# A blank first round of TensorE's loop, split first loads and early branch hints in an attention kernel

## The chip, the cores and the metric

The kernel runs on one core of one Trainium2 chip. The metric is the time of an execution on the device in microseconds (us). Times quoted as a kernel's time are medians of several executions. The profile's span is some 1.5 to 2 us shorter than the same execution's time, because it leaves out what lies before the first and after the last recorded instruction.

## The reference

```python
B, H, Sq, Sk, D = 16, 32, 192, 1024, 128        # q, k, v are bf16

def reference(q, k, v):
    scale = q.shape[-1] ** -0.5
    scores = jnp.einsum("bhqd,bhkd->bhqk", q, k) * scale
    p = _softmax(scores, axis=-1)
    return jnp.einsum("bhqk,bhkd->bhqd", p, v)
```

512 heads, each with 192 queries against 1024 keys. The kernel takes four heads at a time (a group x, 128 groups in all), cuts a group into three pieces, and calls a piece f (384 in all).

## The kernel before

SyncE loads K and V (1 MB each for a group) and Q. VectorE and GpSimd turn K into the layout that the matmul needs, TensorE computes scores (QK), ScalarE the exponentials (e1, e3), TensorE the product with V (PV) four pieces later, VectorE normalises, and the result is stored. The code that the change touches is this, with cuts marked.

```python
            def _(e):                                    # SyncE: the loads
                def load_k(x):
                    if x >= NKN:                         # NKN = 5 buffers
                        e.wait_ge(s_kx, 3 * (x - NKN) + 3)
                    e.dma_start(kn[:, x % NKN, :],
                        kf[4 * x:4 * x + 4].rearrange("a (j r) d -> (a j) (r d)", r=32).bitcast(U32),
                    ).then_inc(s_kn[x % NKN], 16)
                # ... load_q, load_v alike
                k0 = kf[0:4].rearrange("a (j s t) d -> (a j) s (t d)", s=4, t=8).bitcast(U32)
                # ...
                e.dma_start(kn0[:, :, 0:cut], k0[:, :, 0:cut]).then_inc(s_k0, 16)
                load_q(0)
                e.dma_start(kn0[:, :, cut:], k0[:, :, cut:]).then_inc(s_kn[0], 16)
                load_k(1)
                # ... the loads of the following groups, then all the rest, the last stores
                for so in range(NSO):
                    e.wait_ge(s_st[so], 16 * len(range(so, len(stores), NSO)))
```

TensorE's program is one loop of 64 rounds. Each round holds two groups (six pieces). The second half of one PV stands at the head of the next round, so that the jump back falls inside a PV:

```python
                with nc.Fori(0, NF // (3 * R), engines=[mybir.EngineType.PE],
                             head_slot={mybir.EngineType.PE: 100}):
                    pv(-1 - LAG, (1,))
                    for f in range(3 * R):
                        qk(f)
                        pv(f - LAG, (0,) if f == 3 * R - 1 else (0, 1))
```

At the end a flag says whether some row sum was out of range. Each engine loads the flag and branches over a general path that recomputes everything; the branch is taken here:

```python
            with eng.register() as r:
                eng.reg_load(r, redo[0:1, 0:1])
                with eng.If_ne(r, 0):
                    body(eng)
```

## Time and profile before

| kernel before | value |
|---|---|
| time, median of 3 runs | 828.15 us (826.99 to 828.18) |
| span of the profile | 826.16 us |
| first exponential of piece f9 starts at | 38.25 us |
| one round of TensorE's loop, median | 12.420 us |
| from the flag (VectorE's last conversion) to the end of the span | 6.71 us |

I use the start, the rounds and the tail as the ledger. The start of f9 says how well the start went: by then the instructions and the first groups are there, so what comes after is the steady loop. The round is read from the loop's counter instruction, which runs once a round. The tail is what comes after all the work is done. A group line of the profile gives busy time and the mean of one instruction in ns, and after the second bar the idle time just before such instructions with what ended most of it.

### The profile page before, as it was taken

The page shows a single profiled execution, that of the slowest core. Times are in us where ns is not written, and L with a number is a line of the kernel's source. Part 1 is how long each engine was busy: PE and PEld are TensorE (multiplying, and loading weights), DVE is VectorE, ACT ScalarE, POOL GpSimd, SP SyncE. Part 2 cuts the span into 40 slices and gives each one's busy share as a digit, 9 for nine tenths or more (in the row PEclk, how much of TensorE's full clock was granted, in tenths as well). Part 3 has the DMA queues.
Part 4 walks back from the last instruction along what each step waited for, and adds up shares of the span by engine and source line. Part 5 has one row for each costly group of instructions (what it writes and reads, how often), then busy time and mean ns, then how long its engine had stood idle before and what let it go on. Part 6 is the DMA issues. An engine that isn't in the chain of part 4 may idle for free. (4 is left out here: it accounts for less than half of the span.)

```text
span 826.2 us, 71554 instructions
## 1 busy us (share of the span) xinstructions
PE 807.5 (98%) x32926; PEld 717.1 (87%) x32926; DVE 599.8 (73%) x1288; ACT 748.5 (91%) x770; POOL 550.4 (67%) x646
## 2 busy tenths in 40 slices
PE   6899999999999999999999999999999999999995
PEld 4788888888888888888888888888888888888885
DVE  5477777777777777777777777777777777777773
ACT  5699999999999999999999999999999999999994
POOL 6566766766766666667667667666676676676671
PEclk9899999999999999999999999999999999999998
DMA  8999999999999999999999999999999999999951
GB/s 326 398 405 406 406 406 406 407 405 407 407 404 407 405 406 405 403 404 405 401 401 406 399 405 400 399 402 405 399 402 400 403 400 404 397 401 401 402 167 44
DMA packets 139214, 319.22 MB, mean 386 GB/s; under 512 B 7200, under 2 KB 57376, under 8 KB 122912
## 3 DMA queue, kind: packets, MB, share of 16 engines
q1 hardware_dynamic: 106432, 294.41, 91.0%
q10 hardware_dynamic: 32736, 24.38, 8.8%
q14 instruction: 40, 0.33, 0.1%
q8 instruction: 6, 0.10, 0.1%
HBM read 293.60 MB, written 25.17 MB: 386 GB/s over the span
## 5 line engine op out<-in xcount | busy, mean ns | idle before, releaser
L783 ACT ACTIVATE f_pt<-f_s 128x1536 bf16<-128x1536 f32 x384 | 554.6, 1444 | 3.3 <-PE f_o L636 3.3
L571 POOL COPY f_kt<-f_kx 128x768 uint32<-128x768 uint32 (+1 forms) x384 | 294.0, 785 | 255.6 <-DVE f_kx L699 137.3
L636 PE MATMUL f_o<-f_vp,f_pt 128*64 128x129 bf16 x12336 | 424.9, 222 | 3.4 <-issue 3.3
L614 PE MATMUL f_s<-f_qt,f_kt 32*128 32x192 bf16 (+2 forms) x20480 | 422.0, 226 | 5.6 <-PEq L597 3.4
L636 PEld LDWEIGHTS f_o<-f_vp,f_pt 128*64 128x64 bf16 x12336 | 365.3, 110 | 54.7 <-issue 25.5
L614 PEld LDWEIGHTS f_s<-f_qt,f_kt 32*128 32x128 bf16 x20480 | 347.5, 92 | 42.1 <-issue 6.5
L699 DVE STREAM_TRANSPOSE f_kx<-f_kn 128x768 uint32<-128x768 uint32 (+1 forms) x384 | 334.1, 871 | 10.1 <-DMA f_kn<-in_k_dram 10.1
L780 ACT ACTIVATE f_pt<-f_s 128x512 bf16<-128x512 f32 x384 | 229.3, 597 | 62.0 <-PE f_s L614 32.3
L580 POOL COPY f_vp<-f_vs 128x1024 uint32<-128x1024 uint32 x256 | 259.7, 1044 | 5.0 <-PE f_o L636 4.8
L720 DVE RECIPROCAL f_rinv<-f_o 128x2 f32<-128x2 f32 x381 | 65.1, 171 | 192.9 <-PE f_o L636 192.9
L724 DVE TENSOR_TENSOR f_ob<-f_o,f_rinv 128x256 bf16<-128x256 f32 x381 | 161.7, 424 | 13.3 <-DVE f_rinv L720 0.3
L708 DVE STREAM_TRANSPOSE f_qt<-f_qn 128x384 uint32<-128x384 uint32 x128 | 72.8, 569 | 0.0
L661 PE MATMUL f_o<-f_ones 128*128 128x512 bf16 x12 | 4.2, 528 | 1.1 <-POOL f_ones L562 1.1
L661 PEld LDWEIGHTS f_o<-f_ones 128*128 128x128 bf16 x12 | 1.5, 130 | 3.3 <-issue 1.9
L563 POOL MEMSET f_vp<- 128x4352 uint32 x1 | 3.7, 3729 | 0.0
L680 DVE MEMSET f_pt<- 128x3072 uint32 x1 | 2.6, 2618 | 1.5 <-PEq L811 1.5
L636 PE MATMUL f_s<-f_vp,f_pt 128*64 128x129 bf16 x96 | 3.1, 220 | 0.4 <-PEq L597 0.4
L636 PEld LDWEIGHTS f_s<-f_vp,f_pt 128*64 128x64 bf16 x96 | 2.8, 110 | 0.5 <-issue 0.5
L772 ACT ACTIVATE f_pt<-f_ones 128x3072 f32<-128x3072 bf16 x1 | 2.8, 2762 | 0.0
L772 ACT ACT_TABLE_LOAD x1 | 1.3, 1283 | 0.8 <-PEq L811 0.8
L720 DVE RECIPROCAL f_rinv<-f_s 128x2 f32<-128x2 f32 x3 | 0.5, 171 | 1.4 <-PE f_s L636 1.4
L674 PE MATMUL f_o<-f_bad,f_ones 128*1 128x1 bf16 x1 | 0.2, 164 | 1.3 <-DVEq L764 1.3
(13 smaller groups left out, 5.3 us busy)
## 6 DMA issues: line engine op xcount, KB each, us to landing
f_vs<-in_v_dram SPq DMA_DIRECT2D x128, 1024.0 KB, 10.9
f_kn<-in_k_dram SPq DMA_DIRECT2D x127, 1024.0 KB, 13.2
f_qn<-in_q_dram SPq DMA_DIRECT2D x128, 192.0 KB, 13.1
out_dram<-f_ob ACTq DMA_DIRECT2D x62, 384.0 KB, 9.5
f_kn<-in_k_dram SPq DMA_DIRECT2D x1, 640.0 KB, 7.0
f_kn<-in_k_dram SPq DMA_DIRECT2D x1, 384.0 KB, 3.9
out_dram<-f_ob SPq DMA_DIRECT2D x1, 384.0 KB, 3.3
out_dram<-f_ob SPq DMA_DIRECT2D x2, 192.0 KB, 2.1
```

The source lines that it names most:

```text
L571: gp.tensor_copy(kt[:, x % NKT].bitcast(U32).rearrange("p U (j s u) c -> p U j s (u c)", s=2, u=2)[:, lo:hi], kx[:, x % 2].rearrange("p (U ...
L580: gp.tensor_copy(vp[:, x % NVP, 2 * T * i: 2 * T * i + 2 * T, 0:D].bitcast(U32), vs[:, x % NVS, 2 * i: 2 * i + 2, :].rearrange("p a (t d) ...
L614: ins = pe.matmul(S[:, c0: c0 + n1 - n0], kt[r, x % NKT, 2 * t + h, :, c], qt[r, x % R, h, n0:n1, c], start=w == 0 and g == 0, stop=w == 3 ...
L636: return pe.matmul(O[m0: m0 + m, u, 0:129], pt[:, x % R, 2 * y + z, t * SQ + n0: t * SQ + n0 + m], vp[:, x % NVP, (2 * y + z) * T + t, 0:129],
L661: pe.matmul(o_ps[:].rearrange("p a b -> p (a b)"), ones[:], ones[:].unsqueeze(1).to_broadcast([128, 4, 128]), start=True, stop=True)
L699: dve.transpose(kx[:, x % 2].rearrange("p (U s j u) -> p s u U j", s=2, j=32, u=2)[:, :, :, lo:hi], kn[:, x % NKN].rearrange("p (s u U i) ...
L708: dve.transpose(qt[:, x % R].bitcast(U32).rearrange("p b (y j u) c -> p u y b (j c)", y=3, u=2), qn[:, x % NKN].rearrange("p (u y b i) -> ...
L720: dve.reciprocal(ri, O[:, :, 128]).then_inc(s_rc, 1)
L724: dve.tensor_tensor(ob[:, so, 6 * a + 2 * w: 6 * a + 2 * w + 2, :], O[:, :, 0:128], ri.unsqueeze(2).to_broadcast([128, 2, D]), ALU.mult,). ...
L772: act.activation(pt[:, 1].rearrange("p a c -> p (a c)").bitcast(F32), ones[:, 0:1].to_broadcast([128, 2 * T * SQ]), ACT_FN.Copy).then_inc( ...
L780: act.activation(pt[:, x % R, 0, c], s1_ps[:], ACT_FN.Exp, scale=scale).then_inc(s_e1, 1)
L783: act.activation(pt[:, x % R, 1:4, c], s3_ps[f % 2][:], ACT_FN.Exp, scale=scale).then_inc(s_e3, 1)
```

## The change

There are three intents. TensorE's loop gets one more round at first, which does no work: it jumps from the head to a label in the middle and from there to one at the end, in order to have the instruction blocks fetched before the DMA queues fill. The first loads are cut (K in halves, V in quarters), K of the first group becomes an ordinary load, and the first Q goes out on ScalarE's queue. At the end, each engine gets a branch hint well ahead of its branch, and SyncE waits for the last stores after its branch instead of before it. Two waits move along: TensorE's for Q to the loop's head, and the one for the tiles that are filled at the start from TensorE to VectorE. The diff, cut to its core:

```diff
-                with eng.If_ne(r, 0):
+                eng.br_ne(r, 0, on_true=name + "_do", on_false=name + "_end").branch_hint(hints[eng.engine])
 ...
+            sync_general(e)
+            stored(e)
 ...
+    SPLIT_K, SPLIT_V = 2, 4
 ...
+                    n = SPLIT_K if x < NKN else 1
+                    for i in range(n):
+                        e.dma_start(
+                            kn[128 // n * i: 128 // n * (i + 1), x % NKN, :],
+                            kf[4 * x + 4 // n * i: 4 * x + 4 // n * (i + 1)].rearrange(
+                                "a (j r) d -> (a j) (r d)", r=32).bitcast(U32),
+                        ).then_inc(s_kn[x % NKN], 16)
 ...
+                            vs[:, x % NVS, 4 // n * i: 4 // n * (i + 1), :],
 ...
+                load_k(0)
                 load_k(1)
 ...
+                pe.reg_mov(first, 1)
+                def skip(here, there):
+                    pe.br(here)
+                    nc.switch_bb(here, parent=top[0])
+                    pe.br_ne(first, 0, on_true=there, on_false=here + "_on")
+                    nc.switch_bb(here + "_on", parent=top[0])
 ...
-                with nc.Fori(0, NF // (3 * R), engines=[mybir.EngineType.PE],
+                with nc.Fori(0, NF // (3 * R) + 1, engines=[mybir.EngineType.PE],
                              head_slot={mybir.EngineType.PE: 100}):
+                    skip(tag + "_open", tag + "_mid")        # "_mid" lies inside the QK of f4
+                    take(s_qt, 1)
                     pv(-1 - LAG, (1,))
                     for f in range(3 * R):
                         qk(f)
                         pv(f - LAG, (0,) if f == 3 * R - 1 else (0, 1))
+                    nc.switch_bb(tag + "_close", parent=top[0])
+                    pe.reg_mov(first, 0)
+                hint(pe)
```

More of the change, by code (lines that the diff above doesn't have):

```diff
@@ L13, with _only_if, _general_path @@
 R_W = 2
-def _only_if(redo):
+def _only_if(nc, redo, hints):
     def wrap(body):
         def run(eng):
+            name = "redo_%d" % nc.next_id()
             with eng.register() as r:
                 eng.reg_load(r, redo[0:1, 0:1])
-                with eng.If_ne(r, 0):
+                eng.br_ne(r, 0, on_true=name + "_do", on_false=name + "_end").branch_hint(hints[eng.engine])
+                with nc.body(name + "_do", valid_engines=[eng.engine]):
                     body(eng)
+                    eng.br(name + "_end")
+                nc.switch_bb(name + "_end")
         return run
     return wrap
-def _general_path(nc, q, k, v, out, redo, G=16, NS=2, LAGS=(2, 4, 5, 7), ROUTES=(R_W, R_W, R_EA)):
+def _general_path(nc, q, k, v, out, redo, hints, stored, G=16, NS=2, LAGS=(2, 4, 5, 7), ROUTES=(R_W, R_W, R_EA)):
     B, H, SQ, D = q.shape
@@ L142, in wait_evac, with sync_general @@
                 eng.wait_ge(s_eva, ev_cnt[u])
-        @block.sync
-        @_only_if(redo)
-        def _(e):
+        @_only_if(nc, redo, hints)
+        def sync_general(e):
+            stored(e)
             def loads(g):
@@ L186, in _ @@
                 e.wait_ge(sst[so], 48 * n_uses)
+        @block.sync
+        def _(e):
+            sync_general(e)
+            stored(e)
         @block.gpsimd
-        @_only_if(redo)
+        @_only_if(nc, redo, hints)
         def _(gp):
@@ L210, in _ @@
         @block.tensor
-        @_only_if(redo)
+        @_only_if(nc, redo, hints)
         def _(pe):
@@ L308, in _ @@
         @block.vector
-        @_only_if(redo)
+        @_only_if(nc, redo, hints)
         def _(dve):
@@ L362, in _ @@
         @block.scalar
-        @_only_if(redo)
+        @_only_if(nc, redo, hints)
         def _(act):
@@ L442, in _attention_kernel @@
         s_one = sem("f_one")
-        s_k0 = sem("f_k0")
         s_kn = [sem("f_kn%d" % i) for i in range(NKN)]
@@ L511, in _attention_kernel, with load_q, hint @@
             store_at = {3 * (x + c) + 6: i for i, (x, c) in enumerate(stores) if 3 * (x + c) + 6 < NF}
+            def load_q(e, x):
+                e.dma_start(
+                    qn[:, x % NKN, :],
+                    qf[4 * x:4 * x + 4].rearrange("a (j u) d -> (a j) (u d)", u=6).bitcast(U32),
+                ).then_inc(s_qn[x % NKN], 16)
+            hints = {}
+            def hint(eng):
+                hints[eng.engine] = eng.mark_branch_hint_location()
             @block.sync
@@ L517, in load_k @@
                         e.wait_ge(s_kx, 3 * (x - NKN) + 3)
-                    e.dma_start(
-                        kn[:, x % NKN, :],
-                        kf[4 * x:4 * x + 4].rearrange("a (j r) d -> (a j) (r d)", r=32).bitcast(U32),
-                    ).then_inc(s_kn[x % NKN], 16)
-                def load_q(x):
-                    e.dma_start(
-                        qn[:, x % NKN, :],
-                        qf[4 * x:4 * x + 4].rearrange("a (j u) d -> (a j) (u d)", u=6).bitcast(U32),
-                    ).then_inc(s_qn[x % NKN], 16)
+                    n = SPLIT_K if x < NKN else 1
+                    for i in range(n):
+                        e.dma_start(
+                            kn[128 // n * i: 128 // n * (i + 1), x % NKN, :],
+                            kf[4 * x + 4 // n * i: 4 * x + 4 // n * (i + 1)].rearrange(
+                                "a (j r) d -> (a j) (r d)", r=32).bitcast(U32),
+                        ).then_inc(s_kn[x % NKN], 16)
                 def load_v(x):
@@ L531, in load_v @@
                         e.wait_ge(s_pv, 3 * (x - NVS) + 2 + BLANK)
-                    e.dma_start(
-                        vs[:, x % NVS, :, :],
-                        vf[4 * x:4 * x + 4].rearrange("a (m t) d -> m a (t d)", t=T),
-                    ).then_inc(s_v[x % NVS], 16)
-                k0 = kf[0:4].rearrange("a (j s t) d -> (a j) s (t d)", s=4, t=8).bitcast(U32)
-                kn0 = kn[:, 0].rearrange("p (s w) -> p s w", s=4)
-                cut = 32 * PIECES[0][1]
-                e.dma_start(kn0[:, :, 0:cut], k0[:, :, 0:cut]).then_inc(s_k0, 16)
-                load_q(0)
-                e.dma_start(kn0[:, :, cut:], k0[:, :, cut:]).then_inc(s_kn[0], 16)
+                    n = SPLIT_V if x < NVS else 1
+                    for i in range(n):
+                        e.dma_start(
+                            vs[:, x % NVS, 4 // n * i: 4 // n * (i + 1), :],
+                            vf[4 * x + 4 // n * i: 4 * x + 4 // n * (i + 1)].rearrange("a (m t) d -> m a (t d)", t=T),
+                        ).then_inc(s_v[x % NVS], 16)
+                load_k(0)
                 load_k(1)
-                load_q(1)
+                load_q(e, 1)
                 for n in range(2, NKN):
@@ L547, in _ @@
                     load_k(n)
-                    load_q(n)
+                    load_q(e, n)
                 for n in range(NQ):
+                    if n == NQ // 2:
+                        hint(e)
                     if n + NKN - 2 < NQ:
@@ L553, in _, with stored @@
                         load_k(n + NKN)
-                        load_q(n + NKN)
+                        load_q(e, n + NKN)
                 for i in range(len(store_at), len(stores)):
                     store(e, i)
+            def stored(e):
                 for so in range(NSO):
@@ L577, in spread @@
                     if i == 0:
-                        gp.wait_ge(s_v[x % NVS], 16 * (x // NVS + 1))
+                        gp.wait_ge(s_v[x % NVS], 16 * (x // NVS + SPLIT_V))
                         gp.wait_ge(s_pv, 3 * (x - NVP) + 3 + BLANK)
@@ L585, in _ @@
                 for x in range(NQ + 1):
+                    if x == NQ // 2:
+                        hint(gp)
                     if x < NQ:
@@ L600, in qk @@
                     x, b = divmod(f, 3)
-                    if b == 0:
+                    if f == 3:
                         take(s_qt, 1)
@@ L605, in qk @@
                     ins = None
-                    for group in CUTS[b]:
+                    for gi, group in enumerate(CUTS[b]):
+                        if gi == 1 and f == 4:
+                            skip(tag + "_mid", tag + "_close")
                         for w in range(4):
@@ L662, in _ @@
                               ones[:].unsqueeze(1).to_broadcast([128, 4, 128]), start=True, stop=True)
-                pe.wait_ge(s_set, 3)
-                with nc.Fori(0, NF // (3 * R), engines=[mybir.EngineType.PE],
+                first = pe.alloc_register("f_first")
+                tag = "f_skip_%d" % nc.next_id()
+                pe.reg_mov(first, 1)
+                top = []
+                def skip(here, there):
[4 more added lines that the diff above has]
+                with nc.Fori(0, NF // (3 * R) + 1, engines=[mybir.EngineType.PE],
                              head_slot={mybir.EngineType.PE: 100}):
+                    top.append(nc.cur_bb)
+                    skip(tag + "_open", tag + "_mid")
+                    take(s_qt, 1)
                     pv(-1 - LAG, (1,))
@@ L669, in _ @@
                         pv(f - LAG, (0,) if f == 3 * R - 1 else (0, 1))
+                    pe.br(tag + "_close")
+                    nc.switch_bb(tag + "_close", parent=top[0])
+                    pe.reg_mov(first, 0)
+                hint(pe)
                 pv(NF - 1 - LAG, (1,))
@@ L692, in turn_k @@
                     lo, hi = PIECES[b]
-                    if g == 0:
-                        dve.wait_ge(s_k0, 16)
-                    elif g == 1 or b == 0:
-                        dve.wait_ge(s_kn[x % NKN], 16 * (x // NKN + 1))
+                    if b == 0:
+                        dve.wait_ge(s_kn[x % NKN], 16 * (x // NKN + SPLIT_K))
                     if x >= 2:
@@ L745, in _ @@
                 turn_k(0)
+                dve.wait_ge(s_set, 3)
                 turn_q(0)
@@ L751, in _ @@
                     s = f - LAG - 1
+                    if f == NF // 2:
+                        hint(dve)
                     if s >= 0:
@@ L770, in _ @@
             def _(act):
+                load_q(act, 0)
                 act.wait_ge(s_one, 1)
@@ L775, in _ @@
                     x, b = divmod(f, 3)
+                    if f == NF // 2:
+                        hint(act)
                     act.wait_ge(s_qk, f + 1)
@@ L785, in _ @@
                         store(act, store_at[f])
-        _general_path(nc, q, k, v, out, redo)
+        _general_path(nc, q, k, v, out, redo, hints, stored)
 def bass_standalone__mha_softmax__near_ridge_kernel(
```

## The prediction

> **What bounds the kernel now.** I read four views of the kernel before, in this order: the page, the start in order of time, stretches of the start, and the end.
>
> The page says that TensorE is busy almost throughout and, in the groups, that nobody in the middle waits long:
>
> ```profile
> PE 807.5 (98%) x32926; PEld 717.1 (87%) x32926; DVE 599.8 (73%) x1288; ACT 748.5 (91%) x770; POOL 550.4 (67%) x646
> ...
> q8 instruction: 6, 0.10, 0.1%
> ...
> L699 DVE STREAM_TRANSPOSE f_kx<-f_kn 128x768 uint32<-128x768 uint32 (+1 forms) x384 | 334.1, 871 | 10.1 <-DMA f_kn<-in_k_dram 10.1
> ```
>
> VectorE waits for K for only 10.1 us in all, five times, all before 24 us. After that the loop runs like a clock: one round (two groups of four heads, six f) takes 12.420 us in the records of the loop's counter instruction, with the middle half of the rounds within 2 ns. 64 rounds make 795 us. Within a round TensorE goes from one block of matmuls to the next with pauses of about 0.1 us, so TensorE sets the period; ScalarE has 0.11 to 0.16 us to spare in each f. The row q8 is TensorE's own instruction fetch: 0.10 MB in 6 packets, 16 KB each.
>
> What is not in the loop lies at the two ends. The start, in order of time:
>
> ```profile
> 6.92 1.10 PE L614 MATMUL f_s<-f_qt,f_kt 32*128 32x192 bf16 x48 [1.04 <-PEq L597]
> ...
> 9.20 1.57 DVE L699 STREAM_TRANSPOSE f_kx<-f_kn 128x768 uint32<-128x768 uint32 x2 [3.04 <-DMA f_kn<-in_k_dram]
> ...
> 11.40 1.09 PE L614 MATMUL f_s<-f_qt,f_kt 32*128 32x192 bf16 x64 [2.36 <-PEq L597]
> ...
> 20.58 1.13 PE L636 MATMUL f_o<-f_vp,f_pt 128*64 128x129 bf16 x26 [3.34 <-issue]
> ...
> 27.33 1.36 PE L614 MATMUL f_s<-f_qt,f_kt 32*128 32x128 bf16 x46 [2.10 <-issue]
> ```
>
> Two pauses are called "issue": TensorE waited for nothing that the profile shows. Counting instructions from the loop's head (which is put at slot 100 of a block of 256), they fall exactly at slots 768 and 1024, that is at the borders of blocks 3 and 4, and the four fetch packets of the start stand at 11.58, 18.02, 24.84 and 31.23 us (blocks 2, 3, 4, 5), each taking 1.0 to 1.1 us. So these are missing instructions. The stretches around them show the second cost, the halved clock:
>
> ```profile
> 17.20:20.60 3.40, 0.06 (x4) 0.02 (x2) 2.89 (x4) 0.41 (x1) 2.06 (x4) 1.00 1.04 406
> 20.60:24.00 3.40, 3.40 (x100) 2.99 (x102) 0.96 (x1) 1.86 (x2) 2.44 (x3) 0.58 1.04 393
> ...
> 27.30:30.50 3.20, 3.17 (x78) 2.69 (x77) 0.00 (x0) 1.77 (x2) 1.66 (x2) 0.60 1.05 395
> ```
>
> (The last three columns are the granted clock, the DMA share and GB/s.) The DMA engines are full all the time. At the end:
>
> ```profile
> 818.49 0.37 SPq L505 DMA_DIRECT2D out_dram<-f_ob  x1
> ...
> 819.30 0.15 DVE L766 CAST redo<-f_o 1x1 int32<-1x1 f32 x1 [0.34 <-PE f_o L675]
> ```
> ```profile
> L21 SPq COMPARE_BRANCH  x1: 50/50/50, 821.4 to 821.4; - x1
> ...
> L21 PEldq COMPARE_BRANCH  x1: 4249/4249/4249, 821.6 to 821.6; - x1
> ```
>
> The flag is known at 819.45, but the span ends at 826.16. SyncE waits for the last store until 820.5, all engines meet, load the flag (0.5 us), and TensorE's branch over the general path takes 4.25 us, because its target has to be fetched.
>
> [...] two crossings cost 3.5 and 2.1 us here. [...] block 2 was entered for at about 7.5 us and its packet started at 11.58, 4 us later, against 0.95 us at the idle end (821.55 to 822.5). [...] here it took 76 ns not taken and 208 ns taken.
>
> **The change, part by part.**
>
> *End.* SyncE now branches before it waits for the store, and each engine has a branch hint, so the target should be there. From the flag: meeting 0.4, flag load 0.5, branch about 0.2, second meeting 0.4 gives 819.45 + 1.5 = 821.0, with the last store landed at 820.5. Gain 826.2 - 821.0 = 5.1 us (1 us of it from the moved wait alone).
>
> *Start, instruction fetch.* The blank round jumps to block 3 and then block 4 before data floods the queues, and V loads in quarters and K loads in halves leave shorter queues for a fetch to wait behind. It is not free: a fetch is asked for on arrival (at the end the next block's packet starts 0.7 us after the branch is done), so the two come one after the other. About 1.7 us for the jump, then per fetch 0.95 + about 1.2 in the queue + 1.1 + 1.4 from landing to running (19.1 to 20.6, 25.9 to 27.3) = 4.65 us: the loop proper starts at about 11.0, the first QK at 11.8. Block 2 is still fetched on the way, asked for at 12.6 and usable at 17.3, needed at 15.9: 1.4 us stall. Then 2.07 us per f: f3 19.4, f6 25.6, with up to 1 us lost to the half clock 26.5, f9 26.5 + 6.2 = 32.7. Before, f9 started at 37.1. Gain 4.4 us.
>
> *Start, data.* This gain has a ceiling. Comparing each K landing with its first transpose, K of group 4 landed at 28.76 for a transpose at 33.60, of group 5 at 35.15 for 39.82: 4.7 us to spare, rising slowly to 9 us at the end, since the DMA is saturated at about 400 GB/s. A later transpose holds up VectorE's normalisation, which TensorE needs. K0 in 8 KB pieces instead of 768 and 1280 B may bring the stream forward by 1 us: in 2 to 12 us it moved some 0.8 MB less than full rate. So at most 5.7 us. The whole K0 before the first QK costs nothing then: 1.2 MB land at about 6.3, before the code is there.
>
> *Loop.* Each round gets a register move, two branches not taken and the Q wait moved ahead of the second half of a PV. The middle branch should hide: the sequencer is 0.25 us ahead there. At the back edge it is tight. From the counter instruction on, the taken branch ends at 310 ns; a matmul then starts 55 ns later at the soonest (5.175 to 5.23 at first entry), so 365; the 17th weight load of that PV is due at 401. Only 36 ns are spare, and a move (100 ns to the next), a branch not taken (76) and a wait (some 20 more than the 55) add 196 ns without gaps, 300 with them: a hole of 0.16 to 0.27 us, if they run one after the other. If they overlap with matmuls already queued, nothing. I give the hole 60%, at about 0.2, so 0.12 us on average; 64 x 0.12 = 7.7 us.
>
> Sum: 828.15 - 5.1 - 4.4 + 7.7 = 826.35; the report stands 2 us above the span as before. I say **826**.
>
> **The rivals.**
> 1. *The loop's added control is free.* For: the design splits a PV around the back edge to hide just this, and someone tuned it. Against: the 36 ns. Then 828.15 - 5.1 - 5.7 = 817.
> 2. *The control costs its full serial time.* 64 x 0.27 = 17 us, more than both ends gain: with 4.4 at the start 835.9, with a weak start 838.
> 3. *The blank round gains nothing at the start,* since its two fetches come late behind the loads (4.4 us queueing each instead of 1.2 puts f0 at 14 or later[...]). Then the start gains about 1 us, and the time is near 830.
> 4. *The hints miss on some engine.* Then 1 us of 5.1 remains: 830.
>
> **Range and chances.** The good ends together are 817, the bad ones 838; few of the steps go together fully, so 817 to 837 holds 8 in 10. Faster by 2% would need 811.6, below the ceilings of both ends even with a free loop: 0.03. Slower by 2% is 844.7: the full control cost and no gain at the start: 0.03.
>
> **What would show it.** Right: a last span event about 1.5 us after the flag and no 4 us branch; no "issue" pause at blocks 3 and 4, but one of 1 to 4 us in the third f; fetch packets for 3 and 4 before 9 us; f9 near 32.7; VectorE waiting for K of groups 3 to 5; a round of 12.42 to 12.69 us. Wrong: a round above 12.7, f9 after 37, or a round still of 12.42, which would falsify the hole at the back edge.

Cut from this text, where it is marked, are statements of the hardware that no trace of this case shows. "Here it took" speaks of TensorE's compare-and-branch. The half clock of the text is a granted clock of 0.50, from 21.15 to 24.56 us and from 27.97 to 31.39. The 1.7 us for the jump and the 1.2 us in the queue are estimates of mine; the second assumes that shorter transfers shorten the 4 us that a fetch waited in this trace, which was not shown.

## The result, and the profile after

The changed kernel takes 865.14 us (864.17 to 866.08, four runs) against 828.16 us for the kernel before in the same rounds: ratio 1.0448, with a 95% interval of 1.043 to 1.0466. All runs are fast (none is over 1.5% above the fastest of its kernel). Ratios here are the mean time of one kernel's fast runs over that of the other's of the same rounds, so they are not quite the ratio of the medians. The time is 28 us above the upper end of my range.

The ledger shows where it went:

| | before | after | difference |
|---|---|---|---|
| first exponential of f9 starts | 38.25 | 63.02 | +24.8 |
| from there to the first exponential of f383 | 774.40 | 791.64 | +17.2 |
| one round, median | 12.420 | 12.692 | +0.272 |
| flag to end of span | 6.71 | 2.24 | −4.5 |
| span | 826.16 | 863.69 | +37.5 |

The page of the changed kernel, engine totals, TensorE's instruction queue, and the groups of K's transposes and of the first exponential:

```profile
PE 826.4 (96%) x32926; PEld 725.8 (84%) x32926; DVE 599.8 (69%) x1288; ACT 748.6 (87%) x770; POOL 550.4 (64%) x646
...
q8 instruction: 9, 0.15, 0.1%
...
L738 DVE STREAM_TRANSPOSE f_kx<-f_kn 128x768 uint32<-128x768 uint32 (+1 forms) x384 | 334.0, 870 | 20.4 <-DMA f_kn<-in_k_dram 14.0
L825 ACT ACTIVATE f_pt<-f_s 128x512 bf16<-128x512 f32 x384 | 229.3, 597 | 101.8 <-PE f_s L637 78.7
```

VectorE, ScalarE and GpSimd do the same work in the same busy time as before; only their idle time is longer (ScalarE waited 78.7 us for scores here, 32.3 us before). TensorE is busy 19 us longer for the same matmuls. Only 6.2 us of this lie before f9's first exponential, where the stretches below show a granted clock (the share of TensorE's full clock) of 0.50, which was 0.96 and 0.70. The other 12.7 us lie after it, at a clock of 1.00, and 11.9 of them in PV: the loop jumps back in the middle of a PV, and the recorded matmuls there, 221 ns each on average from 100 to 700 us in both kernels, seem to cover most of the longer pause, so that it counts as busy. Nine instruction packets instead of six come in, although the blank round was meant to make fetching cheaper. VectorE waits for K for 14.0 us instead of 10.1.

TensorE's start in order of time (start, duration, and in brackets the idle time before and what ended it):

```profile
16.88 1.08 PE L659 MATMUL f_o<-f_vp,f_pt 128*64 128x129 bf16 x16 [11.14 <-PEq L618]
...
26.29 1.35 PE L659 MATMUL f_o<-f_vp,f_pt 128*64 128x129 bf16 x21 [5.72 <-issue]
...
35.74 1.68 PE L637 MATMUL f_s<-f_qt,f_kt 32*128 32x128 bf16 x40 [4.07 <-issue]
...
45.34 1.67 PE L659 MATMUL f_o<-f_vp,f_pt 128*64 128x129 bf16 x27 [4.75 <-issue]
...
52.11 1.36 PE L637 MATMUL f_s<-f_qt,f_kt 32*128 32x128 bf16 x47 [1.83 <-issue]
```

The first real matmul starts at 16.88 us. The blank round's two jumps took 5.93 and 8.37 us before it. Then the first real round stops four times for instructions, once at each border of the loop's blocks, for 16.4 us in all (5.72 + 4.07 + 4.75 + 1.83). The kernel before had two such "issue" stops, of 3.34 and 2.10 us.

The DMA side, in stretches of ten microseconds of the same start (columns: busy time of PE, PEld, DVE, ACT and POOL with counts, granted clock, DMA share, GB/s), for the kernel before:

```profile
12.00:22.00 10.00, 6.54 (x244) 5.48 (x232) 5.56 (x8) 5.55 (x6) 6.82 (x9) 0.96 1.03 403
22.00:32.00 10.00, 7.90 (x224) 6.79 (x214) 3.81 (x8) 4.26 (x5) 3.54 (x4) 0.70 1.04 400
```

and for the changed one:

```profile
12.00:22.00 10.00, 3.69 (x75) 3.05 (x76) 3.19 (x5) 2.05 (x2) 3.55 (x5) 0.50 1.05 258
22.00:32.00 10.00, 5.38 (x125) 4.53 (x124) 1.96 (x2) 1.94 (x2) 2.03 (x2) 0.50 1.04 239
```

The DMA engines show as fully busy in both, yet they move only 240 to 260 GB/s in place of 400. A busy share alone does not show this; the last column does. One 8 KB packet took a mean of 607 ns between 12 and 42 us, against 318 ns before.

The end improved. In the changed kernel, the branch over the general path, per engine (durations in ns as min/median/max, then first and last start):

```profile
L22 SPq COMPARE_BRANCH  x1: 75/75/75, 862.7 to 862.7; - x1
...
L22 PEldq COMPARE_BRANCH  x1: 461/461/461, 862.8 to 862.8; - x1
```

TensorE's branch takes 0.461 us where it took 4.249.

### The profile page after: what moved, and what is told of

Same layout as the page of the kernel before. It is cut to its first block, busy times and chain, and to the rows that moved or that the text cites. A ratio compares the mean times of both kernels' runs of the same rounds, so it can differ in the third digit from the quotient of the medians.

```text
span 863.7 us, 71777 instructions
## 1 busy us (share of the span) xinstructions
PE 826.4 (96%) x32926; PEld 725.8 (84%) x32926; DVE 599.8 (69%) x1288; ACT 748.6 (87%) x770; POOL 550.4 (64%) x646
## 5 line engine op out<-in xcount | busy, mean ns | idle before, releaser
L659 PE MATMUL f_o<-f_vp,f_pt 128*64 128x129 bf16 x12336 | 440.3, 223 | 26.2 <-PEq L618 11.1
L659 PEld LDWEIGHTS f_o<-f_vp,f_pt 128*64 128x64 bf16 x12336 | 371.8, 110 | 86.8 <-issue 59.8
L825 ACT ACTIVATE f_pt<-f_s 128x512 bf16<-128x512 f32 x384 | 229.3, 597 | 101.8 <-PE f_s L637 78.7
```

The lines of the kernel that those rows point to most:

```text
L659: return pe.matmul(O[m0: m0 + m, u, 0:129], pt[:, x % R, 2 * y + z, t * SQ + n0: t * SQ + n0 + m], vp[:, x % NVP, (2 * y + z) * T + t, 0:129],
L825: act.activation(pt[:, x % R, 0, c], s1_ps[:], ACT_FN.Exp, scale=scale).then_inc(s_e1, 1)
```

## The experiments

My theory after the comparison was that three losses add: K halves that write only half of the partitions slow the loads (258 GB/s from 12 to 22 us, against 403 before); the blank round costs its jumps (5.93 and 8.37 us) and does not keep what they fetched; and the added control in the loop costs its full serial time (0.272 us a round). The rivals were that the number or size of the transfers is at fault rather than the partitions, that the blank round is harmless once the loads are whole, and that the loop's cost comes from one instruction, or from the middle branch. Eleven kernels ran; all gave correct results.

### K whole again

```diff
-    SPLIT_K, SPLIT_V = 2, 4
+    SPLIT_K, SPLIT_V = 1, 4
```

> The changed kernel with K of the first five groups loaded whole again (one transfer over 128 partitions) in place of two halves of 64 partitions; all else as changed. Theory A (a load that writes only 64 of 128 partitions runs at about half rate, and this starves the start): from 2 to 42 us the queues move 380 to 400 GB/s in place of 230 to 260, the 8 KB packets of the first 12 us take about 370 ns in place of 583, and the time falls by 12 to 20 us to 845 to 853. Rival B (the blank round alone makes the start late, the half loads do no harm): rate and time stay, 862 to 868. The round stays at 12.69 us in both.

Measured: 852.43 us (852.26 to 852.77), ratio 1.0301 (1.0284 to 1.0318). f9 starts at 50.16 us instead of 63.02, the round (12.694) and the tail (2.24) are as in the changed kernel. The same stretch of the start:

```profile
12.00:22.00 10.00, 3.69 (x75) 3.05 (x76) 2.53 (x4) 2.05 (x2) 2.05 (x3) 0.50 1.02 389
```

The rate is back at 389 GB/s, and 12.9 us of the start with it. The start is still 11.9 us worse than before. The stops of the first real round:

```profile
15.16 1.08 PE L659 MATMUL f_o<-f_vp,f_pt 128*64 128x129 bf16 x16 [8.79 <-PEq L618]
...
22.09 1.35 PE L659 MATMUL f_o<-f_vp,f_pt 128*64 128x129 bf16 x21 [3.24 <-issue]
...
28.53 0.98 PE L637 MATMUL f_s<-f_qt,f_kt 32*128 32x128 bf16 x40 [1.14 <-issue]
...
34.91 1.68 PE L659 MATMUL f_o<-f_vp,f_pt 128*64 128x129 bf16 x27 [3.05 <-issue]
```

They show how the halves cost time in the changed kernel: not by late data at TensorE, whose pauses there after the first matmul are all "issue", but by slower fetches. Without the halves the first matmul comes 1.7 us earlier (15.16 instead of 16.88), and the stops are three, of 7.4 us in all, instead of four, of 16.4. That is 10.7 of the 12.9 us.

### K in two, along the rows

The same number of transfers of the same size as in the changed kernel, but each half covers all 128 partitions (the 128 rows of a tile on the chip, the first number of its shape in the profile) and half of each row.

```diff
-                            kn[128 // n * i: 128 // n * (i + 1), x % NKN, :],
+                            kn[:, x % NKN, 2048 // n * i: 2048 // n * (i + 1)],
```

> The changed kernel with K of the first five groups still in two transfers, but each takes half of the rows' bytes in all 128 partitions (4 KB pieces). Theory A (it is the partitions): as with K whole, within 3 us of that run, rate 380 to 400 GB/s. Rival C (it is the number of transfers, or their smaller size): as the changed kernel, 862 to 868, rate 230 to 260 GB/s.

Measured: 853.84 us, ratio 1.0326 (1.0306 to 1.0346), f9 at 49.85 us, 383 GB/s from 12 to 22 us. That is the kernel with whole K, not the one with halves. So neither the number nor the size of the transfers is at fault, but the 64 partitions that each half writes.

### K halves in the kernel before

```diff
+                    n = 2 if 1 <= x < NKN else 1
+                    for i in range(n):
+                        e.dma_start(
+                            kn[128 // n * i: 128 // n * (i + 1), x % NKN, :],
```

(The source and the wait's count follow.)

> The kernel before with one thing of the change: K of groups 1 to 4 in two halves of 64 partitions each (K0 stays in its two pieces over 128 partitions). If half the partitions mean half the rate: the K landings of groups 2, 3 and 4 (17.4, 23.0, 28.8 us before) come about 4, 6 and 8 us later, VectorE waits for them, 8 KB packets of 12 to 42 us take about 580 ns in place of 317, and the time rises by 5 to 9 us to 833 to 837. If the halves hurt only together with the blank round: within 1.5 us of the kernel before.

Measured: 842.46 us (839.98 to 843.34) against 827.68, ratio 1.0173 (1.0147 to 1.0198). The halves alone cost 14.8 us, well over the 5 to 9 us that I expected, with the round unchanged at 12.420. The stretch, and its longest waits (total us, times, longest):

```profile
12.00:22.00 10.00, 7.56 (x230) 6.52 (x230) 3.99 (x6) 4.47 (x5) 3.79 (x5) 0.68 1.05 218
```

```profile
DVE f_kx L702 <- DMA f_kn<-in_k_dram: 28.3, 6, 8.1
...
PE f_o L639 <- issue: 6.3, 1, 6.3
PE f_s L617 <- issue: 5.0, 2, 4.8
```

The direction was right and the size was off for a reason that these lines show: K comes later (28.3 us of waiting instead of 10.1), and TensorE's instruction fetches come later too: the two issue stops grow from 3.34 and 2.10 us to 6.32 and 4.79. V, which is loaded here as before, slows down too: its 2 KB packets took 142 ns on average from 12 to 22 us, against 88 in the kernel before. So the halves slow transfers that were left as they were.

### No blank round

The changed kernel without the two skips and the extra round; the K halves stay.

```diff
-                        if gi == 1 and f == 4:
-                            skip(tag + "_mid", tag + "_close")
-                with nc.Fori(0, NF // (3 * R) + 1, engines=[mybir.EngineType.PE],
+                with nc.Fori(0, NF // (3 * R), engines=[mybir.EngineType.PE],
-                    skip(tag + "_open", tag + "_mid")
-                    pe.br(tag + "_close")
-                    nc.switch_bb(tag + "_close", parent=top[0])
-                    pe.reg_mov(first, 0)
```

> The changed kernel without the blank round: no register, no branches inside the loop, 64 rounds; K halves, V quarters, the wait for Q at the head and the hints stay. Theory A with the round's cost being its control: the round falls from 12.69 to 12.42 to 12.57 us (8 to 17 us in all), the data of the start still come at 230 to 260 GB/s and the start stays late by 10 us or more against the kernel before: 838 to 850 us. Rival B (the blank round makes the start late): the start comes back too, 822 to 832 us.

Measured: 834.5 us (833.99 to 834.93), ratio 1.0086 (1.0069 to 1.0103). f9 starts at 46.15 us, 16.9 earlier than with the blank round, and the round is 12.467 us, 0.225 shorter. That lies between the ranges of both theories (838 to 850, and 822 to 832): the start came back by more than theory A allowed, but not all of it. The blank round with its control is the largest single loss. What stays in the round, 0.047 us over the kernel before, belongs to the wait for Q that now stands ahead of the PV, the only thing in the loop that this kernel still has changed.

### Neither

> The changed kernel with K whole and without the blank round: what stays is V in quarters, K0 in one transfer, q0 from ScalarE's queue, the wait for Q at the loop's head, and the end. The head's wait costs 0.047 us a round (12.467, as without the blank round alone): 3.0 us. If the two culprits (half-partition K loads, blank round) are all that was wrong with the start, the first exp of f9 comes within 1.5 us of the kernel before (38.2 us) and the time is 825 to 828. If the V quarters or the single K0 also cost, f9 is after 40 us and the time over 829; if they help, f9 is before 36.5 and the time under 825.

The edit is "K whole again" and "No blank round" together. Measured: 828.14 us (828.03 to 829.21) against 828.17, ratio 0.9999 (0.9982 to 1.0016). f9 starts at 41.03 us and the round is 12.475. I had put a time over 829 with an f9 after 40; only the f9 came so. So the start, with what stays of the first loads, is 2.8 us worse than before, and the rounds some 3 us; the end gives 4.5 back. The two losses at the start do not simply add: whole K brings 12.9 us with the blank round, and 5.1 without it (46.15 to 41.03).

### The new end alone

The kernel before with only the hints and the moved wait for the stores.

```diff
+                eng.br_ne(r, 0, on_true=name + "_do", on_false=name + "_end").branch_hint(hints[eng.engine])
 ...
+            sync_general(e)
+            stored(e)
```

> The kernel before with only the changed end: SyncE branches before it waits for the last stores, and each engine has its branch hint. If the end is independent of the rest, the tail from the flag to the end of the span is 2.2 us in place of 6.7 and the time 823 to 824.5 us. If the hints cost something elsewhere, or the branch of TensorE misses here, 826 to 828.

Measured: 823.4 us (822.68 to 823.95), ratio 0.9951 (0.9935 to 0.9968). The tail is 2.23 us, the round 12.427, f9 at 37.65 (0.6 us earlier than in the kernel before, with the same start; the next kernel, again with the same start, has 38.60, so this number scatters by about 1 us). This is the part of the change that pays: the version is 0.5% faster than the kernel before, with an interval that leaves out 1. TensorE's branch in it:

```profile
L22 PEldq COMPARE_BRANCH  x1: 482/482/482, 820.5 to 820.5; - x1
```

### The moved wait alone

```diff
-        @_only_if(redo)
-        def _(e):
+        def sync_general(e):
+            stored(e)
 ...
+            sync_general(e)
+            stored(e)
```

> The kernel before with only the moved wait for the last stores, without branch hints. TensorE's branch over the general path still fetches for about 4.2 us. The tail from flag to end falls from 6.7 to about 5.7 us, since the meeting no longer waits for the store that lands 1 us after the flag: 826.5 to 827.5. If the moved wait were the whole gain: 823 to 824.

Measured: 827.04 us (825.75 to 828.39), ratio 0.9991 (0.9969 to 1.0013), so not told from the kernel before by its time. The tail in the trace is 5.88 us instead of 6.71, and TensorE's branch is as long as ever:

```profile
L21 PEldq COMPARE_BRANCH  x1: 4389/4389/4389, 821.1 to 821.1; - x1
```

By these single traces the moved wait is worth 0.8 us of the tail, and the hints the other 3.65 (5.88 to 2.23); without hints TensorE's branch took 4.149 to 4.389 us in three kernels.

### Two blank rounds

With whole K, and the condition on the loop's counter, so that the first two rounds are blank. If the jumps fill the instruction store, the second blank round finds everything there.

```diff
-                    pe.br_ne(first, 0, on_true=there, on_false=here + "_on")
+                    pe.br_lt(first[0], 2, on_true=there, on_false=here + "_on")   # first[0]: the loop's counter
-                with nc.Fori(0, NF // (3 * R) + 1, engines=[mybir.EngineType.PE],
+                with nc.Fori(0, NF // (3 * R) + 2, engines=[mybir.EngineType.PE],
```

> K whole, with two blank rounds in a row (66 rounds; the condition is on the loop's counter, which adds one register move a round). It asks whether a block fetched by a jump is still held. Theory D (a jump to a block that isn't held gives up what was held before it): the second blank round has to fetch again, its branches take some 4 to 6 us each, and the first exp comes 8 to 12 us later than with one blank round (18.1 us). Rival E (blocks 3 and 4 are held, and only blocks 1 and 2 were lost): the second blank round takes under 1.5 us in all, and the start is as with one. The span is one look, about 862 (D) or 852 (E).

Measured in the one look: 862.58 us, f9 at 59.98 us. The second blank round's jumps took 12.07 and 5.70 us. The skip's branches, all of them:

```profile
L694 PEldq COMPARE_BRANCH  x132: 64/64/12072, 1.5 to 848.7; - x132
```

The second round waited again for what the first had jumped to a moment before. Theory D's direction holds, but its 4 to 6 us a branch and 8 to 12 us in all were too low: the first exponential comes at 37.20 us instead of 18.11. In this pattern of jumps, then, a block that was jumped to is not held a round later.

### Stops in order

With whole K and one blank round, but the blank round stops in each of the blocks 1, 2, 3, 4 in turn instead of leaping from 0 to 3 to 4.

```diff
-                        if gi == 1 and f == 4:
-                            skip(tag + "_mid", tag + "_close")
+                        if (f, gi) in VISIT:             # VISIT = [(1, 1), (2, 2), (4, 1), (5, 1)]
+                            n = VISIT.index((f, gi))
+                            skip(tag + "_mid%d" % n, tag + ("_mid%d" % (n + 1) if n + 1 < len(VISIT) else "_close"))
```

> K whole, with a blank round that stops in every block in turn (1, 2, 3, 4) before it closes, so that no block is jumped over; two more branches a round. Theory D (it is the jump over a block that loses what is held): going in order nothing is lost, and the first real round has no pause called issue at a block's border; the blank round itself takes four fetches one after the other, some 20 us, and the first exp is at 24 to 30 us. Rival F (whatever a blank round fetches is lost when the loop goes back to its head): the first real round pauses at all four borders again. The round grows by at most 0.05 us more.

Measured in the one look: 845.38 us, f9 at 43.84 us. The five branches took 0.36, 6.01, 5.71, 6.00 and 0.22 us, and TensorE's start reads:

```profile
20.91 1.08 PE L660 MATMUL f_o<-f_vp,f_pt 128*64 128x129 bf16 x16 [14.86 <-PEq L618]
21.91 1.89 PE L638 MATMUL f_s<-f_qt,f_kt 32*128 32x192 bf16 x48
23.74 1.94 PE L660 MATMUL f_o<-f_vp,f_pt 128*64 128x129 bf16 x32
25.61 1.28 PE L638 MATMUL f_s<-f_qt,f_kt 32*128 32x192 bf16 x64
26.89 1.10 PE L660 MATMUL f_o<-f_vp,f_pt 128*64 128x129 bf16 x32
```

From here on there is no issue stop at any border, and only four fetch packets came in (5.56, 11.18, 17.33 and 23.35 us), as in the kernel before. So in these kernels blocks were kept when they were entered in order, and not when one was leapt over. It still does not pay: three fetches one after the other, near 6 us each, stand before the first matmul, whereas the kernel before works between its fetches. The round is 12.686 us, no longer than the 12.694 of whole K with one middle branch, although it has three more branches that are not taken: such branches in mid-round cost nothing that shows here.

### The loop's counter in place of the register move

With whole K, the loop written by hand, so that the condition reads the counter and the move at the end of each round goes.

```diff
-                    pe.br_ne(first, 0, on_true=there, on_false=here + "_on")
+                    pe.br_eq(first, 0, on_true=there, on_false=here + "_on")
-                    pe.reg_mov(first, 0)
+                    pe.reg_alu(first, first, 1, ALU.add)
+                    pe.br_lt(first, NF // (3 * R) + 1, on_true=tag + "_loop", on_false=tag + "_end")
```

> K whole, the blank round decided by the loop's own counter (the loop written out by hand), so that the register move at the end of each round is gone; two branches not taken and the wait for Q at the head stay. If the control at the back edge runs one after the other, the round falls by the move's 0.097 us from 12.694 to 12.60, 64 rounds are 6.2 us, and the time goes from 852.4 to about 846. If the move overlaps with queued matmuls, round and time stay within 0.02 us and 1.5 us.

Measured: 846.2 us (846.04 to 846.36) against 828.17, ratio 1.0217 (1.02 to 1.0234). The round is 12.6165 us, 0.078 shorter than with the move: 65 moves come to 5 us. Of the blank round's control the open branch at the head and the middle branch are left in it; 12.6165 less the 12.475 of the kernel with neither blank round nor halves is 0.14 us a round. As three more middle branches cost nothing above, I put it on the head, by subtraction and not by a run of its own.

### K of the first group in one transfer

The kernel with the new end alone, plus one edit:

```diff
-                e.dma_start(kn0[:, :, 0:cut], k0[:, :, 0:cut]).then_inc(s_k0, 16)
+                load_k(0)
                 load_q(0)
-                e.dma_start(kn0[:, :, cut:], k0[:, :, cut:]).then_inc(s_kn[0], 16)
```

> The kernel before with the new end (823.4 us) and K0 in one transfer over 128 partitions, everything else of the start as before. Theory G (the first QK comes later, and with it the entry into block 1 that asks for the next fetch, so the whole chain of fetches moves): the first fetch packet is at about 13 to 14 us in place of 11.4, the first exp of f9 at 39.5 to 41.5 in place of 37.7, and the time is 825 to 827. Rival H (the start is bound by K of groups 3 to 5, K0 does not matter, and the late f9 of the run without blank round came from the V quarters): f9 within 0.7 us, 823 to 824.2.

Measured: 825.0 us (824.25 to 825.39), ratio 0.9967 (0.995 to 0.9985), inside the expected 825 to 827; f9 at 39.75 us against 37.65, inside 39.5 to 41.5. Against the new end alone, which ran in another call, both ratios to the kernel before put it 0.0016 apart, 1.3 us, but the intervals overlap; the f9s differ by twice the scatter. The data do come sooner: 379 GB/s from 2 to 12 us instead of 314, and the first transposes of groups 2 and 3 start 1.4 us earlier (16.16 and 21.86 us). The first fetch packet comes later, at 12.57 us instead of 11.41 (I had expected 13 to 14), and so do the next three. So earlier data did not help, and the late start goes with the fetches: the likely reason is that TensorE enters the next block later (its first QK starts at 7.85 us against 6.94), and the chain of fetches starts later.

## Why the prediction was wrong

The loss has three parts, and each answers to a step of mine. The start, by where f9 begins:

| from | to | f9 | step |
|---|---|---|---|
| before | neither halves nor blank round | 38.25 to 41.03 | +2.8 |
| neither | blank round added | 41.03 to 50.16 | +9.1 |
| blank round | K halves added | 50.16 to 63.02 | +12.9 |

**Start, data.** The step that failed most is the one that is not there. I listed the K halves only as shorter queue entries and put the ceiling of the start from K's slack at a rate of "about 400 GB/s", without asking where each half lands. The halves write partitions 0 to 63 or 64 to 127. What such a transfer moves I had not measured. The trace shows it: 232 GB/s from 2 to 12 us, where K's 8 KB packets are 90% of the bytes (378 with K whole), and 206 and 204 GB/s in two stretches where they are 71% and 56%, the rest being Q and V:

```profile
16.00:22.00 6.00, 3.69 (x75) 3.05 (x76) 1.08 (x3) 2.05 (x2) 1.58 (x3) 0.50 1.00 206
26.00:32.00 6.00, 5.38 (x125) 4.53 (x124) 0.98 (x1) 1.94 (x2) 2.03 (x2) 0.50 1.04 204
```

The two halves of a group were issued one after the other, and the measured rate shows that they did not add up to that of one whole transfer. I also expected K0 in 8 KB pieces to "bring the stream forward by 1 us". The last experiment shows that it did, by 1.4 us, and that f9 came about 2 us later all the same, with the later fetches. The remaining 0.7 us of the 2.8 is within the scatter of f9; what the V quarters, Q's other queue or the moved waits do to it I did not take apart.

**Start, instruction fetch.** "V loads in quarters and K loads in halves leave shorter queues for a fetch to wait behind", with "about 1.2 in the queue": wrong. In the kernel with whole K, the first matmul of a new block ran at 22.09 us and the next fetch packet came at 26.01, 3.9 us later; in the kernel before, with V in one piece, it was 4.3 and 3.9 (20.58 to 24.84, 27.33 to 31.23). With the halves it was 6.5 and 6.9 (26.29 to 32.82, 35.74 to 42.59), so they made the wait longer, where the step had them make it shorter. And the step took for granted that a block that was jumped to is then held. It was not: of the four borders of the changed kernel's first real round, none was free, including the border of block 1, which the kernel before passed without a packet and without a stop. The loop proper was to start at 11.0 us, with the packets of blocks 3 and 4 before 9; they came at 4.60 and 13.38, and the loop started at 16.1. I expected the QK of f9 at 32.7 (its exponential follows 1.15 us later); it starts at 61.88 in the changed kernel, and at 49.01 with K whole. Rival 3, that the blank round gains nothing, pointed this way, but allowed it no loss of its own: its two jumps took some 14.3 us in the changed kernel and then bought nothing. Of my signs of being wrong, "f9 after 37" came true.

**Loop.** The mechanism was right and the size was off. The term was a hole of 0.16 to 0.27 us, taken at 60% as 0.12; it measured 0.272, the full serial value of rival 2, and 64 rounds make 17.4 us, where I had 7.7. The parts: the move 0.078, the Q wait 0.047 to 0.055, and the rest, some 0.14, goes by subtraction with the branch at the head. The middle branch hides, as I said (12.686 us a round with four of them, 12.694 with one). The 0.14 us of the head is not the duration of its branch: single compare-and-branches took 63 to 76 ns not taken, and 208 taken. The back edge had only 36 ns to spare, and I had worked that out; the error was to give instructions that run on one sequencer, one after the other, a 40% chance to cost nothing.

**End.** Right: 5.1 us predicted, 4.5 measured (6.71 to 2.24), with the branch at 0.461 us. I put 1 us of it on the moved wait, and it is 0.8. Rival 4 falls. The last event comes 2.24 us after the flag rather than 1.5, because the first meeting of all engines and TensorE's branch were dearer than I took them: the flag's loads start 0.6 to 0.8 us after it was known (I had 0.4), and the branch takes 0.46 (I had 0.2).

**Sum.** With the measured terms it reads 828.15 + 24.8 + 17.2 − 4.5 = 865.65, against 865.14; as the terms come from traces of the same two kernels, this checks only that none is missing. Rivals 2 and 3 came together, and the halves came on top, which no rival had.

**What stays open.** In the kernel before, TensorE fetched nothing from 31.23 us until its loop was over near 812 us (the next packet came at 816.06), though a round runs over slots 100 to beyond 1024, and the two stops, at slots 768 and 1024, put a block at 256 slots; so five blocks at least were held at once. Why a jump over a block then left four stops in the changed kernel's next round (three with K whole), while entering the blocks in order left none, I did not settle; I have only these two patterns. And why the halves cost 5.1 us in f9 without the blank round, but 12.9 with it and 14.7 in the kernel before (38.25 to 52.98), I did not settle; the rates from 22 to 32 us differ too (277, 239 and 225 GB/s). The number of fetches that come while the rate is low goes some way: without the blank round, the first matmul (8.27 to 10.62 us) and the stops (6.6 to 8.4 us) account for 4.1 of the 5.1 us, as they do for 10.7 of the 12.9 with it.

## What to carry to other kernels

When a load is cut, cut it so that each part still covers all 128 partitions (383 against 258 GB/s here), and check GB/s rather than the DMA's busy share. Don't count on warming the instruction store by jumping ahead: here the jumps came one after the other and took 5.93 and 8.37 us (5.7 to 6.0 each when stopping in order), and four stops, of 16.4 us in all, followed in the next round. A hint well ahead of a branch took it from 4.25 to 0.46 us. In a loop whose period one engine sets, count each control instruction at its back edge at full cost, times the rounds (0.272 us, 64 times, here), unless a run shows otherwise. The hints and the moved wait alone gave 823.4 us, faster than both kernels.
